# Moving 18 of 64 key rows per partition from ScalarE's row sums to VectorE's adder tree in a decode-attention kernel

## The chip, the cores and the metric

The kernel runs on one core of one Trainium2 chip. The metric is device time in microseconds (us). All the runs of one kernel here agree within 0.3%, and the record marks them all as fast (undisturbed), so they are compared as they are. A core has TensorE (matmul), VectorE, ScalarE, GpSimd, SyncE (which issues the loads here) and 16 DMA engines.

## The reference, cut to what matters

Two independent attention blocks, A and B, each with 2 batches, 32 heads, one query row, 8192 cached keys and head size 192, all in bf16:

```python
q = (x @ wq).reshape(B, Sq, H, Dh).transpose(0, 2, 1, 3)
scores = jnp.einsum("bhqd,bhkd->bhqk", q, k_cache) * (Dh ** -0.5)
p = softmax(scores, axis=-1)
o = jnp.einsum("bhqk,bhkd->bhqd", p, v_cache)
out = o.transpose(0, 2, 1, 3).reshape(B, Sq, H * Dh) @ wo     # A and B are concatenated
```

Every K and V element is read once and used once: 128 units (block, head, batch) of 3072 KB of K and 3072 KB of V, 805 MB in all.

## The kernel before: the parts that matter

A unit's 8192 keys lie as 64 rows of 192 elements in each of 128 partitions. The score of a row is the sum of 192 products. VectorE multiplies all rows by the query, in two instructions. The first `na` rows (28) go to ScalarE, which sums each with one `activation` whose `accum_out` is the score; in the trace this is two instructions a row (3582 ACTIVATE and 3582 ACTIVATION_READ_ACCUMULATOR for the 3582 rows of the kernel before). The other 36 rows VectorE sums itself, by halving 192 to 96, 48 and 24 columns and one reduce.

```python
def dve_d1a(u):      # products for ScalarE
    na = na_of(u)
    return lambda eng: eng.tensor_tensor(prodA[u % 2][:, 0:na, :], kb[u % NK][:, 0:na, :], qb_bc(u, na), ALU.mult)
def dve_d1b(u):      # products for VectorE; when it is done, K's buffer is free
    ...              # rows na..T into prodD
def dve_d3(u):       # the maximum over all 64 scores of a partition
    return lambda eng: eng.tensor_reduce(mp[u % 2][:], sc[u % 2][:], AXL.X, ALU.max)
def dve_lvl(u, w):   # w = 96, 48, 24
    nd = T - na_of(u)
    return lambda eng: eng.tensor_tensor(prodD[:, 0:nd, 0:w], prodD[:, 0:nd, 0:w], prodD[:, 0:nd, w:2 * w], ALU.add)
def dve_r(u):        # the reduce over 24 columns
    ...
def act_acc(u, t):   # ScalarE: one row
    return lambda eng: eng.activation(prodA[u % 2][:, t, :], prodA[u % 2][:, t, :], ACTF.Identity,
                                      accum_out=sc[u % 2][:, t:t + 1])
...
for t in range(na_of(u)):
    put(act_tab, u, 10 + t, act_acc(u, t), ...)
```

After the maximum come GpSimd's cross-partition maximum, ScalarE's exponentials and 32 TensorE matmuls against V. K and V have two buffers each. SyncE issues the loads in order: the K load of unit u waits for `d1b` of unit u-2, the V load for the matmuls of unit u-2. The program has no loops; every instruction of the 128 units stands in it.

## Time and profile before

| | before |
|---|---|
| time, median | 2008.2 us (2008.0 to 2008.6, 3 runs) |
| DMA | 838 MB, 418 GB/s on average |
| VectorE, ScalarE, TensorE busy | 74%, 72%, 56% |
| loads in flight | about 3: 23 to 24 us from issue to landing, one landing every 7 to 8 us |

These are lines of the page of the profile of before: busy us by engine (part 1), GB/s in 40 equal slices of the span (part 2), the DMA queues with packets, MB and share of the 16 engines' time (part 3), and the chain that ended last (part 4).

```profile
PE 1116.4 (56%) x5014; PEld 592.4 (30%) x5014; DVE 1484.8 (74%) x962; ACT 1435.5 (72%) x7811; POOL 143.6 (7%) x270
...
GB/s 389 429 428 431 430 429 431 429 431 427 428 426 426 423 413 430 419 425 420 420 430 407 424 420 418 429 411 428 416 417 433 413 423 422 410 433 414 430 417 235
...
q1 hardware_dynamic: 55856, 836.79, 98.8%
q8 instruction: 39, 0.64, 0.1%
q14 instruction: 75, 0.61, 0.1%
...
DMA 74%; PE 20%; DVE 4%; ACT 2%; issue 0%; POOL 0%; SPq 0%
DMA vb<-in_A_v_cache_dram 38%; DMA vb<-in_B_v_cache_dram 22%; PE ops L344 19%; DMA kb<-in_B_k_cache_dram 13%; DVE prodD L251 2%; DVE prodA L247 2%; ACT prodA L269 1%; DMA kb<-in_A_k_cache_dram 1%; POOL mg L234 0%; PE outps L379 0%; PE oTps L363 0%; PE oTps L352 0%; SPq L187 0%; SPq L194 0%; ACT pb L276 0%
```

DMA bounds the kernel: it leads the chain that ended last with 74%, and its engines are busy 0.9 or more in 39 of 40 slices. But look at the slices: after the first, twelve move 426 to 431 GB/s, and later ones fall to 407 to 420 again and again.

The groups of instructions that the change touches (line, engine, operation, out<-in, shapes, count | busy us, mean ns of one | idle us just before them and what ended it), before:

```profile
L269 ACT ACTIVATE prodA<-prodA 128x192 bf16<-128x192 bf16 x3582 | 1239.7, 351 | 238.3 <-DVE prodA L247 238.2
...
L247 DVE TENSOR_TENSOR prodA<-kb,qbc 128x5376 bf16<-128x5376 bf16 x128 | 378.5, 2957 | 281.4 <-DMA kb<-in_A_k_cache_dram 142.5
L251 DVE TENSOR_TENSOR prodD<-kb,qbc 128x6912 bf16<-128x6912 bf16 x128 | 480.4, 3753 | 1.2 <-DMA kb<-in_A_k_cache_dram 1.2
L258 DVE TENSOR_TENSOR prodD<-prodD 128x3456 bf16<-128x3456 bf16 (+2 forms) x384 | 464.8, 1210 | 13.3
L254 DVE TENSOR_REDUCE mp<-sc 128x1 f32<-128x64 f32 x128 | 28.2, 220 | 201.4 <-ACT prodA L269 201.3
```

VectorE waits for K 281 us in total and for ScalarE's last row 201 us (line L254).

### The profile page before, as it was taken

To read this page: it belongs to the slowest core of one execution; us is meant where nothing else is said; L and a number is where in the kernel's file an instruction comes from. 1 tells how busy PE (TensorE), PEld (TensorE's weight loads), DVE (VectorE), ACT (ScalarE), POOL (GpSimd) and SP (SyncE) were. 2 spreads that over 40 slices of the span, in tenths; PEclk is the share of its full clock that TensorE was granted. 3 is DMA by queue.
4 is the path that set the end of the run, shared out by engine and by line. 5 is a ranking of instruction groups with operands and counts; after the bars stand their busy time and mean duration, and the time that the engine had idled before them with its cause. 6 is when DMAs were issued, how large, how long until landed. Compare 5 with 4: busy or idle time off the path is not lost.

```text
span 2005.8 us, 19822 instructions
## 1 busy us (share of the span) xinstructions
PE 1116.4 (56%) x5014; PEld 592.4 (30%) x5014; DVE 1484.8 (74%) x962; ACT 1435.5 (72%) x7811; POOL 143.6 (7%) x270
## 2 busy tenths in 40 slices
PE   2565555556555565556654565546655565555557
PEld 1232323223232233223322333223332233222323
DVE  7777877877777777777777767777677776877676
ACT  6776777767767676776767767777677776777776
POOL 2000100000000001000000000000000020000001
PEclk9776777777777777777777777777777777777778
DMA  9999999999999999999999999999999999999995
GB/s 389 429 428 431 430 429 431 429 431 427 428 426 426 423 413 430 419 425 420 420 430 407 424 420 418 429 411 428 416 417 433 413 423 422 410 433 414 430 417 235
DMA packets 55986, 838.05 MB, mean 418 GB/s; under 512 B 7352, under 2 KB 18240, under 8 KB 22848
## 3 DMA queue, kind: packets, MB, share of 16 engines
q1 hardware_dynamic: 55856, 836.79, 98.8%
q8 instruction: 39, 0.64, 0.1%
q14 instruction: 75, 0.61, 0.1%
q10 hardware_dynamic: 16, 0.01, 0.0%
HBM read 836.77 MB, written 0.01 MB: 417 GB/s over the span
## 4 chain that ended last, share of the span: by engine, by line
DMA 74%; PE 20%; DVE 4%; ACT 2%; issue 0%; POOL 0%; SPq 0%
DMA vb<-in_A_v_cache_dram 38%; DMA vb<-in_B_v_cache_dram 22%; PE ops L344 19%; DMA kb<-in_B_k_cache_dram 13%; DVE prodD L251 2%; DVE prodA L247 2%; ACT prodA L269 1%; DMA kb<-in_A_k_cache_dram 1%; POOL mg L234 0%; PE outps L379 0%; PE oTps L363 0%; PE oTps L352 0%; SPq L187 0%; SPq L194 0%; ACT pb L276 0%
## 5 line engine op out<-in xcount | busy, mean ns | idle before, releaser
L344 PE MATMUL ops<-vb,pb 128*33 128x384 bf16 x4096 | 954.1, 408 | 880.1 <-DMA vb<-in_A_v_cache_dram 451.2
L269 ACT ACTIVATE prodA<-prodA 128x192 bf16<-128x192 bf16 x3582 | 1239.7, 351 | 238.3 <-DVE prodA L247 238.2
L344 PEld LDWEIGHTS ops<-vb,pb 128*33 128x33 bf16 x4096 | 481.9, 120 | 1352.8 <-issue 1207.4
L269 ACT ACTIVATION_READ_ACCUMULATOR prodA<-prodA 128x1 f32 x3582 | 680.7, 190 | 0.0
L247 DVE TENSOR_TENSOR prodA<-kb,qbc 128x5376 bf16<-128x5376 bf16 x128 | 378.5, 2957 | 281.4 <-DMA kb<-in_A_k_cache_dram 142.5
L251 DVE TENSOR_TENSOR prodD<-kb,qbc 128x6912 bf16<-128x6912 bf16 x128 | 480.4, 3753 | 1.2 <-DMA kb<-in_A_k_cache_dram 1.2
L258 DVE TENSOR_TENSOR prodD<-prodD 128x3456 bf16<-128x3456 bf16 (+2 forms) x384 | 464.8, 1210 | 13.3
L254 DVE TENSOR_REDUCE mp<-sc 128x1 f32<-128x64 f32 x128 | 28.2, 220 | 201.4 <-ACT prodA L269 201.3
L234 POOL PARTITION_ALL_REDUCE mg<-mp x128 | 50.2, 392 | 1734.0 <-DVE mp L254 1734.0
L262 DVE TENSOR_REDUCE sc<-prodD 128x36 f32<-128x864 bf16 x128 | 134.8, 1053 | 4.4
L283 ACT ACTIVATE o_sb<-ops 1x384 f32<-1x384 f32 x63 | 30.3, 480 | 123.8 <-PE oTps L352 95.7
L311 ACT ACTIVATE qbc<-qps 128x384 bf16<-128x384 f32 x64 | 31.4, 491 | 92.5 <-PE qps L332 92.5
L273 ACT ACTIVATE nb<-mg 128x1 f32<-128x1 f32 x128 | 26.0, 203 | 99.5 <-POOL mg L234 99.5
L238 POOL PARTITION_ALL_REDUCE lall<-rs x128 | 85.8, 670 | 103.0 <-ACT pb L276 103.0
L352 PEld LDWEIGHTS oTps<-ones,o_sb 33*128 33x128 f32 x372 | 67.1, 257 | 9.8 <-issue 9.8
L352 PE MATMUL oTps<-ones,o_sb 33*128 33x1 f32 x372 | 69.8, 311 | 0.0
L276 ACT ACTIVATE pb<-sc,nb 128x64 bf16<-128x64 f32 x128 | 52.2, 408 | 4.3 <-ACT nb L273 0.2
L332 PE MATMUL qps<-wqs,xbc_0 128*128 128x384 bf16 x160 | 32.5, 335 | 6.1 <-DMA wqs<-in_A_wq_dram 6.1
L332 PE MATMUL qps<-wqs,xbc_1 128*128 128x384 bf16 x160 | 32.4, 334 | 0.6 <-ACT qbc L311 0.6
L379 PE MATMUL outps<-wos,oTz 128*4 128x320 bf16 x192 | 32.1, 304 | 0.1
L284 ACT ACTIVATE o_sb<-ops 1x384 f32<-1x384 f32 x63 | 30.4, 482 | 0.7
L276 ACT ACTIVATION_READ_ACCUMULATOR pb<-sc,nb 128x1 f32 x128 | 23.9, 187 | 0.0
(30 smaller groups left out, 84.8 us busy)
## 6 DMA issues: line engine op xcount, KB each, us to landing
vb<-in_A_v_cache_dram SPq DMA_DIRECT2D x64, 3072.0 KB, 23.0
kb<-in_A_k_cache_dram SPq DMA_DIRECT2D x63, 3072.0 KB, 24.0
kb<-in_B_k_cache_dram SPq DMA_DIRECT2D x63, 3072.0 KB, 23.8
vb<-in_B_v_cache_dram SPq DMA_DIRECT2D x62, 3072.0 KB, 23.2
wos<-in_A_wo_dram SPq DMA_DIRECT2D x8, 960.0 KB, 25.1
wqs<-in_B_wq_dram SPq DMA_DIRECT2D x8, 960.0 KB, 27.5
wos<-in_B_wo_dram SPq DMA_DIRECT2D x8, 960.0 KB, 25.1
wqs<-in_A_wq_dram SPq DMA_DIRECT2D x7, 960.0 KB, 27.5
```

The lines of the kernel that those rows point to most:

```text
L234: return lambda eng: eng.partition_all_reduce(mg[u % 2][:], mp[u % 2][:], 128, bass.bass_isa.ReduceOp.max)
L238: return lambda eng: eng.partition_all_reduce(lall[g % 2][:, b:b + 1], rs[u % 2][:], 128, bass.bass_isa.ReduceOp.add)
L247: return lambda eng: eng.tensor_tensor(prodA[u % 2][:, 0:na, :], kb[u % NK][:, 0:na, :], qb_bc(u, na), ALU.mult)
L251: return lambda eng: eng.tensor_tensor(prodD[:, 0:T - na, :], kb[u % NK][:, na:T, :], qb_bc(u, T - na), ALU.mult)
L258: return lambda eng: eng.tensor_tensor(prodD[:, 0:nd, 0:w], prodD[:, 0:nd, 0:w], prodD[:, 0:nd, w:2 * w], ALU.add)
L262: return lambda eng: eng.tensor_reduce(sc[u % 2][:, na:T], prodD[:, 0:T - na, 0:24], AXL.X, ALU.add)
L269: return lambda eng: eng.activation(prodA[u % 2][:, t, :], prodA[u % 2][:, t, :], ACTF.Identity, accum_out=sc[u % 2][:, t:t + 1])
L276: return lambda eng: eng.activation(pb[u % 2][:, :, ::32], sc[u % 2][:].rearrange("p (j a) -> p j a", a=2), ACTF.Exp, bias=nb[u % 2][:], s ...
L332: ins = eng.matmul(qps[:, 0:QW], xbc[blk][b][:, c, :], wqs[w % 2][:, c, off:off + QW], start=(c == 0), stop=(c == DC - 1))
L344: ins = eng.matmul(ops[(u // B) % 2][0:33, b, 0:QW], pb[u % 2][:, j, :], vv[:, j, :], start=(j == 0), stop=(j == T // 2 - 1))
L352: ins = eng.matmul(oTps[:, 2 * i + b:2 * i + b + 1], o_sb[:, b, :, :].rearrange("p s (r i) -> p i (s r)", i=3)[:, i, :], ones33[:], start= ...
L379: ins = eng.matmul(outps[0:4, 0:NH2], oTz[pp % 2][:, i, 2 - 2 * half:6 - 2 * half], wos[w % 2][:, pr, i, half * NH2:(half + 1) * NH2], sta ...
```

## The change

The intent is to relieve ScalarE, whose 28 rows end after VectorE's tree. The whole diff:

```diff
-    NA_MAIN = min(cfg.get("NA", 28), T - 2)
+    NA_MAIN = min(cfg.get("NA", 10), T - 2)
     NA_LAST = min(cfg.get("NA_LAST", 26), T - 2)
```

127 units now give ScalarE 10 rows and VectorE 54. The last unit keeps 26 and 38.

## The prediction

> **What bounds the kernel now.** The DMA stream of the K and V caches. In the page's slices the DMA engines are busy 0.9 or more in 39 of 40; the windows view gives a DMA share of 1.00 at 426-430 GB/s in mid-run. 838 MB at 418 GB/s is the whole span of 2005.8 us, or 15.67 us for each of the 128 units (one head and batch, K and V 3072 KB each). A load takes 23-24 us from issue to landing while one lands about every 7.3 us: about three are in flight. In the waits view VectorE waits for K 281 us in 126 waits (2.2 us a unit), TensorE for V 879 us. [...]

> **What the change does, per unit** (127 of 128; the last keeps its own 26/38 split).
> - VectorE, by line fits through the sizes in the trace: the two products 2.96+3.75 us become about 1.17+5.54 (sum unchanged); the tree levels 1.96+1.06+0.61 become 2.86+1.51+0.84; the reduce 1.05 becomes about 1.50. Busy 11.6 -> about 13.7 us, total 1485 -> about 1755 us, 87-88% of the span.
> - ScalarE loses 18 accumulate pairs of 0.345 us, 6.2 us a unit: busy 1435 -> about 645 us, 32%.
> - VectorE's maximum waited for ScalarE's last row (201 us, 1.6 us a unit). That goes, so from K's landing to the maximum's end only lengthens from about 13.2 to 13.8 us.
> - K's buffer comes free after both products, 6.7 us after landing as before. Bytes don't change, but for some 4,600 fewer ScalarE instructions to fetch.

> **On the critical path.** Next to nothing. The shortest K-to-K periods in the timeline are 14.60 us; VectorE needs about 13.9 with gaps, so it still waits for K, some 0.7 us there, more elsewhere. V lands 7.4 us after the next K, so softmax weights 0.6 us later are still early.

> The end does matter: after the last K the chain runs through unit 126's 28 ScalarE rows and unit 127's 26. For unit 126 VectorE's tree now comes last: its maximum, and the last unit's start, about 0.7 us later. Expect +0.5 to +1 us. At the start unit 0's tree delays unit 1 by about 2.5 us while loads are queued: absorbed.

> **Predicted: 2008.6 us, 8 in 10 between 2003 and 2014.** Faster by over 2%: 0.01; within 2%: 0.96; slower by over 2%: 0.03.

> **What would show it.** VectorE 87-88%, ScalarE about 32%; DMA 9 in all slices but the last, about 418 GB/s; VectorE's wait for ScalarE's rows gone; its wait for K around 1.7 us a unit (some 200 us); TensorE's waits for V about as before; the chain of waits still led by DMA, with unit 126's ScalarE rows out of the tail.

> **What would make it wrong.** (1) The longer tree runs slower than the fits, past 14.6 us: then VectorE paces the short periods. (2) With little idle time behind the maximum, GpSimd's cross-partition maximum collides with the next product. [...] the trace shows such a GpSimd reduction taking 2.8-3.0 us instead of 0.35-0.39. Behind the second product it could be 5.5, and the weights late for V; three loads in flight should hide it. (3) The DMA rate differing with engine traffic, which nothing here suggests.

No term of the forecast's sum is among them: it has next to nothing in the stream and +0.5 to +1 us in the tail, and comes to 2008.6 us against 2008.2 before.

## The result, and the profile after

| | before | after |
|---|---|---|
| time, median | 2008.1 us (4 runs) | 1981.3 us (1980.0 to 1981.7, 4 runs) |
| ratio | | 0.9868 (0.9854 to 0.9882) |
| DMA | 838.05 MB at 418 GB/s | 837.75 MB at 423 GB/s |
| VectorE, ScalarE busy | 74%, 72% | 88%, 32% |

A ratio is the mean time of one kernel's fast runs over that of the other's in the same rounds, so it is not quite the ratio of the medians. The kernel gained 1.3%, 27 us; the prediction was 2008.6 us and its range ended at 2003. The same lines of the page, after:

```profile
PE 1123.6 (57%) x5014; PEld 595.2 (30%) x5014; DVE 1741.8 (88%) x962; ACT 640.7 (32%) x3239; POOL 165.9 (8%) x270
...
GB/s 389 428 429 432 429 428 431 430 431 428 428 433 429 430 430 429 432 430 429 430 430 430 430 430 430 429 429 431 429 425 431 428 430 430 425 430 427 430 428 224
...
q1 hardware_dynamic: 55856, 836.79, 99.1%
q8 instruction: 39, 0.64, 0.1%
q14 instruction: 39, 0.32, 0.0%
...
DMA 75%; DVE 23%; PE 1%; ACT 1%; issue 0%; POOL 0%; SPq 0%; DVEq 0%
DMA kb<-in_B_k_cache_dram 39%; DMA kb<-in_A_k_cache_dram 37%; DVE prodD L251 18%; DVE prodA L247 4%; DVE prodD L258 1%; ACT prodA L269 0%; PE ops L344 0%; DVE sc L262 0%; POOL mg L234 0%; PE outps L379 0%; PE oTps L363 0%; SPq L187 0%; SPq L194 0%; DVE mp L254 0%; ACT pb L276 0%
```

The load bytes (q1) are the same to the last digit. The low slices are gone: but for the first and the last, none is below 425 GB/s. The one queue that differs is q14: 39 packets instead of 75. The groups after:

```profile
L251 DVE TENSOR_TENSOR prodD<-kb,qbc 128x10368 bf16<-128x10368 bf16 x128 | 709.0, 5539 | 3.8 <-DMA kb<-in_A_k_cache_dram 3.8
L258 DVE TENSOR_TENSOR prodD<-prodD 128x5184 bf16<-128x5184 bf16 (+2 forms) x384 | 664.8, 1731 | 13.3
L269 ACT ACTIVATE prodA<-prodA 128x192 bf16<-128x192 bf16 x1296 | 449.2, 352 | 63.6 <-DVE prodA L247 62.9
...
L247 DVE TENSOR_TENSOR prodA<-kb,qbc 128x1920 bf16<-128x1920 bf16 x128 | 149.9, 1171 | 186.6 <-DMA kb<-in_B_k_cache_dram 93.1
...
L254 DVE TENSOR_REDUCE mp<-sc 128x1 f32<-128x64 f32 x128 | 28.1, 220 | 9.0 <-ACT prodA L269 1.0
```

VectorE and ScalarE did what was predicted: 1742 us against 1755, 641 against 645, the wait for rows 201 us down to 1, the wait for K 187 us against "some 200".

**Where the time came from: K's landings.** VectorE starts a unit's first product as soon as K has landed (of units 3 to 126, 123 of 124 before and all 124 after start 0.02 us behind the landing), so its starts show when loads land. The timeline of before, VectorE alone (start us, duration us, instruction, [idle before <-releaser]):

```profile
226.70 2.96 DVE L247 TENSOR_TENSOR prodA<-kb,qbc 128x5376 bf16<-128x5376 bf16 x1 [2.26 <-DMA kb<-in_A_k_cache_dram]
...
241.31 2.96 DVE L247 TENSOR_TENSOR prodA<-kb,qbc 128x5376 bf16<-128x5376 bf16 x1 [1.58 <-DMA kb<-in_A_k_cache_dram]
...
256.58 2.96 DVE L247 TENSOR_TENSOR prodA<-kb,qbc 128x5376 bf16<-128x5376 bf16 x1 [0.32 <-DMA kb<-in_A_k_cache_dram]
...
271.21 2.96 DVE L247 TENSOR_TENSOR prodA<-kb,qbc 128x5376 bf16<-128x5376 bf16 x1 [1.59 <-DMA kb<-in_A_k_cache_dram]
```

The distances are 14.61, 15.27 and 14.63 us. From unit 3 to 126 most distances (94 of 123, to 0.05 us) have one of four values: 14.60; 14.60 + 0.67; 16.91, when a weight load of 960 KB comes between; and that + 0.67. The DMA view of before in the first of these windows (226.70 to 241.31) lists one queue, in the second (241.31 to 256.58) two:

```profile
q1 hardware_dynamic: 288, 6.29, 100.4%
```

```profile
q1 hardware_dynamic: 297, 6.51, 99.6%
q14 instruction: 1, 0.01, 0.1%
```

One 8 KB packet of instructions fell into the longer distance. The longer window also moved more bytes, 6.51 MB against 6.29: K landed later, but most of the stream did not stop. Not every such packet costs: the third distance, 14.63 us (256.58 to 271.21), holds one too and is not longer:

```profile
q1 hardware_dynamic: 509, 6.29, 101.3%
q8 instruction: 1, 0.02, 0.4%
q14 instruction: 1, 0.01, 0.1%
```

After the change such distances still exist, but are rarer. Timeline of after:

```profile
699.09 1.16 DVE L247 TENSOR_TENSOR prodA<-kb,qbc 128x1920 bf16<-128x1920 bf16 x1 [0.84 <-DMA kb<-in_A_k_cache_dram]
...
713.67 1.16 DVE L247 TENSOR_TENSOR prodA<-kb,qbc 128x1920 bf16<-128x1920 bf16 x1 [0.68 <-DMA kb<-in_A_k_cache_dram]
...
728.96 1.16 DVE L247 TENSOR_TENSOR prodA<-kb,qbc 128x1920 bf16<-128x1920 bf16 x1 [1.51 <-DMA kb<-in_A_k_cache_dram]
```

From 699.09 to 713.67 (14.58 us) the DMA view of after has one packet of q8, from 713.67 to 728.96 (15.29 us) one packet of q14:

```profile
q1 hardware_dynamic: 287, 6.27, 100.4%
q8 instruction: 1, 0.02, 0.5%
```

```profile
q1 hardware_dynamic: 301, 6.56, 100.2%
q14 instruction: 1, 0.01, 0.1%
```

Sorting the distances of before this way, from unit 3 to unit 126: with no instruction packet in the window they exceed 14.60 (or 16.91) by 0.03 us on average (38 of them), with one packet of q8 alone by 0.06 (18), with one packet of q14 alone by 0.62 (45). The queues can be named by counting. The compiled programs have 7959 instructions for ScalarE before and 3387 after; VectorE's has 1103, GpSimd's 286, SyncE's 311, TensorE's 10202, all unchanged. The 4572 ScalarE instructions that are gone took 36 packets of 8 KB off q14, 127 each; at 128 to a packet, the first four programs fill 75 packets before and 40 after: q14 (75 and 39). The 13716 TensorE instructions added in run 9 below brought 54 packets of 16 KB more on q8, 254 each; at 256 to a packet TensorE's 10202 fill 40: q8 (39).

**The balance.** From the first product of unit 3 to that of unit 126 before takes 1910.7 us and after 1882.6: 28.1 us gained. The start gives 0.2 more. The tail, from unit 126's K to the end, loses 2.2 (40.2 to 42.4 us). Together 26.1, the difference of the spans (2005.8 and 1979.7).

The tail's loss has two parts. Unit 126's tree delays the last softmax by 0.74 us (the last 32 matmuls start 27.81 us behind unit 126's first product instead of 27.07). And these matmuls take 7.05 us instead of 5.38. The windows view gives the clock granted to TensorE in that stretch (columns: stretch, length, busy us of PE, PEld, DVE, ACT, POOL, PEclk, DMA share, GB/s), for before

```profile
1992.60:1998.10 5.50, 5.42 (x34) 3.16 (x34) 0.16 (x1) 2.06 (x8) 0.39 (x1) 1.00 0.03 13
```

and for after

```profile
1965.10:1972.30 7.20, 7.12 (x34) 3.72 (x34) 0.16 (x1) 2.08 (x8) 0.39 (x1) 0.76 0.01 5
```

so 1.00 before and 0.76 after. Why the clock differs there was not tried.

### The profile page after: what moved, and what is told of

Read it like the earlier page. It is cut to its first block, busy times and chain, and to the rows that moved or that the text cites. A ratio compares the mean times of both kernels' runs of the same rounds, so it can differ in the third digit from the quotient of the medians.

```text
span 1979.7 us, 15250 instructions
## 1 busy us (share of the span) xinstructions
PE 1123.6 (57%) x5014; PEld 595.2 (30%) x5014; DVE 1741.8 (88%) x962; ACT 640.7 (32%) x3239; POOL 165.9 (8%) x270
## 2 busy tenths in 40 slices
DMA packets 55950, 837.75 MB, mean 423 GB/s; under 512 B 7352, under 2 KB 18240, under 8 KB 22976
## 4 chain that ended last, share of the span: by engine, by line
DMA 75%; DVE 23%; PE 1%; ACT 1%; issue 0%; POOL 0%; SPq 0%; DVEq 0%
DMA kb<-in_B_k_cache_dram 39%; DMA kb<-in_A_k_cache_dram 37%; DVE prodD L251 18%; DVE prodA L247 4%; DVE prodD L258 1%; ACT prodA L269 0%; PE ops L344 0%; DVE sc L262 0%; POOL mg L234 0%; PE outps L379 0%; PE oTps L363 0%; SPq L187 0%; SPq L194 0%; DVE mp L254 0%; ACT pb L276 0%
## 5 line engine op out<-in xcount | busy, mean ns | idle before, releaser
L251 DVE TENSOR_TENSOR prodD<-kb,qbc 128x10368 bf16<-128x10368 bf16 x128 | 709.0, 5539 | 3.8 <-DMA kb<-in_A_k_cache_dram 3.8
L258 DVE TENSOR_TENSOR prodD<-prodD 128x5184 bf16<-128x5184 bf16 (+2 forms) x384 | 664.8, 1731 | 13.3
L269 ACT ACTIVATE prodA<-prodA 128x192 bf16<-128x192 bf16 x1296 | 449.2, 352 | 63.6 <-DVE prodA L247 62.9
L247 DVE TENSOR_TENSOR prodA<-kb,qbc 128x1920 bf16<-128x1920 bf16 x128 | 149.9, 1171 | 186.6 <-DMA kb<-in_B_k_cache_dram 93.1
L269 ACT ACTIVATION_READ_ACCUMULATOR prodA<-prodA 128x1 f32 x1296 | 246.9, 190 | 0.0
L262 DVE TENSOR_REDUCE sc<-prodD 128x54 f32<-128x1296 bf16 x128 | 192.0, 1500 | 4.4
L238 POOL PARTITION_ALL_REDUCE lall<-rs x128 | 106.3, 831 | 102.3 <-ACT pb L276 102.3
L254 DVE TENSOR_REDUCE mp<-sc 128x1 f32<-128x64 f32 x128 | 28.1, 220 | 9.0 <-ACT prodA L269 1.0
L284 ACT ACTIVATE o_sb<-ops 1x384 f32<-1x384 f32 x63 | 30.4, 482 | 0.7
```

Source lines behind the costliest of these rows:

```text
L238: return lambda eng: eng.partition_all_reduce(lall[g % 2][:, b:b + 1], rs[u % 2][:], 128, bass.bass_isa.ReduceOp.add)
L251: return lambda eng: eng.tensor_tensor(prodD[:, 0:T - na, :], kb[u % NK][:, na:T, :], qb_bc(u, T - na), ALU.mult)
L262: return lambda eng: eng.tensor_reduce(sc[u % 2][:, na:T], prodD[:, 0:T - na, 0:24], AXL.X, ALU.add)
```

## The experiments

Theories at the start. **A**: each block of 128 ScalarE instructions that is fetched holds the K and V stream up by about 0.67 us. **B**: ScalarE's time was the cause; its rows delayed the softmax and the release of V. **C**: the instruction bytes of any engine cost the stream. After the first four runs A was replaced by **M**: of the programs on q14 only the longest costs, and the others hide behind it.

All kernels of a call ran on one chip beside runs of before, whose medians were 2007.3 to 2008.1 us; so medians may be compared across calls to about 1 us. Every kernel passed the comparison with the reference (for the fifth run see there).

### 1: ScalarE's instructions without ScalarE's work

From the kernel after. The added instructions test a semaphore that is long satisfied; the compiler puts two tests into one instruction (72 tests a unit in 127 units make 4572 instructions more).

```diff
+            for t in range(72 if u < NU - 1 else 0):
+                put(act_tab, u, 60 + t, lambda eng: eng.wait_ge(S_dve.sem, 1), [], None)
```

> The changed kernel plus 36 ScalarE instructions in each of 127 units, which do nothing but test a semaphore that is long satisfied; they stand behind the rows, and ScalarE's program is as long as before the change (7959 instructions). Theory A (each 8 KB block of 128 ScalarE instructions that is fetched holds the K/V stream up by about 0.67 us): 36 blocks more, so 2005 us (2000 to 2010), the instruction queue q14 back at 75 packets, K-to-K periods of 15.3 us as frequent as before. Rival B (the gain came from ScalarE's time: its 28 rows delayed the maximum, the softmax and so the release of V): no time to speak of is added, 1981 to 1984. Rival C (any engine's instruction bytes cost the stream): 2005 as well.

Measured: 2009.8 us, ratio to before 1.0013 (0.9998 to 1.0028). The gain is gone. Lines of its page:

```profile
PE 1116.4 (56%) x5014; PEld 592.9 (30%) x5014; DVE 1741.7 (87%) x962; ACT 640.3 (32%) x3239; POOL 145.5 (7%) x270
...
q14 instruction: 75, 0.61, 0.1%
```

VectorE and ScalarE are as busy as after the change, and q14 is as before it. The stream from unit 3 to 126 takes 1910.1 us (before 1910.7). This is A or C; B falls. The time is 2 us above before for the tail, whose last 32 matmuls take 6.96 us here too.

### 2: ScalarE's work without its instructions

From the kernel after: after the last row, four passes over all ten rows in place (the identity), each waiting for the one before, and the maximum waits for the last.

```diff
+                for t in range(4):
+                    put(act_tab, u, 60 + t, act_same(u), [("same", u, t - 1) if t else ("rows", u)],
+                        ("acc", u) if t == 3 else ("same", u, t))
```

> The changed kernel plus four long ScalarE passes over its own ten rows per unit (results unchanged), about 7 us, and VectorE's maximum waits for the last: ScalarE about as busy as before the change or more, but with 508 more instructions instead of 4572. Theory A and C: 4 blocks more, 1984 us (1981 to 1987). Rival B: the gain is lost, 2000 to 2010.

Measured: 1983.7 us, ratio 0.9883 (0.9868 to 0.9897). ScalarE is busier than before the change, and the gain stays but for the four blocks. From its page:

```profile
PE 1104.8 (56%) x5014; PEld 589.1 (30%) x5014; DVE 1741.2 (88%) x962; ACT 1555.6 (78%) x3747; POOL 218.7 (11%) x270
...
q14 instruction: 43, 0.35, 0.0%
```

VectorE's maximum waited for these passes only 39 us in total, so the wait itself is restored in part only. But in the kernel after, unit 126's maximum starts later behind its first product than before anyway (13.56 us against 12.81), and the kernel is faster.

### 3: GpSimd's instructions

As the first, with `pool_tab` and slot `u + 1` in place of `act_tab` and `u`.

> As the first, but the 4572 instructions stand in GpSimd's program. Theory A (only ScalarE's fetches cost; the few q14 packets of the changed kernel that cost nothing are as many as VectorE's, GpSimd's and SyncE's programs fill): 1981 us (1979 to 1985), q14 at 75 packets. Rival C (any instruction bytes): 2005. Rival B: 1981.

Measured: 1988.1 us, ratio 0.9904 (0.9889 to 0.9918). Between A and C, and the pattern says why. Of its timeline:

```profile
716.10 1.16 DVE L247 TENSOR_TENSOR prodA<-kb,qbc 128x1920 bf16<-128x1920 bf16 x1 [0.68 <-DMA kb<-in_A_k_cache_dram]
...
731.35 1.16 DVE L247 TENSOR_TENSOR prodA<-kb,qbc 128x1920 bf16<-128x1920 bf16 x1 [1.47 <-DMA kb<-in_A_k_cache_dram]
...
745.95 1.16 DVE L247 TENSOR_TENSOR prodA<-kb,qbc 128x1920 bf16<-128x1920 bf16 x1 [0.81 <-DMA kb<-in_A_k_cache_dram]
```

From unit 12 to 123, 35 distances are long like the 15.25 us here, one every 3.3 units. GpSimd's program, 4858 instructions, fills a block every 128 / (4858 / 128) = 3.4 units, ScalarE's 3387 one every 4.8. In the kernel after, long distances come every 4.9 units from unit 17 on, and in the first run about every 2.1 (7959 instructions fill one every 2.06). So in this run GpSimd's blocks cost and ScalarE's no longer do: most of the windows that hold a q14 packet without being longer would be theirs, which the views don't show. This led to M.

### 4: TensorE's instructions

```diff
+            if u < NU - 1:
+                put(pe_tab, u, 0.5, pe_small(18), [("init",)], None)   # 18 matmuls of 16 columns, unused
```

> The changed kernel plus 18 small matmuls a unit (36 TensorE instructions) into an unused PSUM bank: 4572 more TensorE instructions, about 18 more packets of 16 KB on q8. Theory A (TensorE's fetches showed no cost in either trace): 1981 us (1979 to 1986). Rival C: 2000 to 2010. Rival B: 1981.

Measured: 1980.1 us, ratio 0.9864 (0.9847 to 0.988), 57 packets on q8 (39 after, 1981.3 us). TensorE's fetches are free here; C falls.

### 5: The row split of before with half of ScalarE's instructions

From the kernel before: ScalarE sums two rows at once. The scores are then wrong on purpose (the comparison with the reference did not notice).

```diff
-eng.activation(prodA[u % 2][:, t, :], prodA[u % 2][:, t, :], ACTF.Identity,
+eng.activation(prodA[u % 2][:, t:t + n, :], prodA[u % 2][:, t:t + n, :], ACTF.Identity,   # n = 2, t even
```

> The kernel before (28 rows a unit on ScalarE, 36 on VectorE), but ScalarE sums two rows in one instruction, so 28 ScalarE instructions a unit fewer; the result is wrong on purpose. ScalarE's program falls from 7959 to 4404 instructions, 62 to 34 blocks, VectorE's part is untouched. Theory M (new: of all the instruction programs only the one with the most 8 KB blocks costs, about 0.67 us a block; the others hide behind it): 28 blocks fewer, 1989 us (1984 to 1993). Rival B' (VectorE's longer share of rows is what helped): 2007.

Measured: 1984.0 us, ratio 0.9881 (0.9866 to 0.9895). VectorE works exactly as before (1484.8 us busy), so its larger share of the rows is not what helps. The 5 us below the centre are explained below: a block fewer saves nearer 0.8 us than 0.67.

### 6: The additions of runs 1 and 3 together

> The changed kernel plus 36 instructions a unit in ScalarE's program and 36 in GpSimd's, the additions of the first and third run together: 62 and 38 blocks. Theory M: as ScalarE's alone, 2010 us (2006 to 2013), GpSimd's blocks hidden. Rival S (each program adds its own cost, 28 us and 7 us over the changed kernel): 2017 or more.

Measured: 2008.2 us, ratio 1.0002 (0.9987 to 1.0017), with

```profile
q14 instruction: 111, 0.91, 0.1%
```

111 packets cost no more than the 75 of run 1 (2009.8 us). The costs of two programs do not add. M holds, S falls.

### 7 and 8: The change taken further

Run 7 sets `NA` to 2. Run 8 gives VectorE all 64 rows in one product (`NA_MAIN = 0`, the first product left out, unit 0's K load unsplit).

> The change taken further: ScalarE sums 2 rows a unit, VectorE 62. ScalarE's program has 1355 instructions, 11 blocks instead of 26; VectorE's busy time rises to about 14.6 us a unit, against K-to-K periods of 14.60 us and 15.2 us on average. Theory M: 1971 us (1967 to 1976). Rival V (VectorE, now 95% busy, paces the short periods): 1980 or more.

> All 64 rows on VectorE in one product, but for the last unit; ScalarE's program has 847 instructions, 7 blocks, so VectorE's 1039 (8 blocks) are now the most. Theory M: 1970 us (1966 to 1976), a us of it a later last unit. Rival V: 1982 or more, VectorE 97% busy. If ScalarE's blocks alone cost: 1968.

Measured: 1973.7 us (ratio 0.9828, 0.9812 to 0.9844) and 1974.2 us (0.9832, 0.9818 to 0.9847). Both lie in their ranges, and the eighth is not better than the seventh. VectorE is busy 94 and 95% and leads the chain of waits with 56 and 58%; from run 7 to run 8, two more rows moved to VectorE gained nothing (1973.7 and 1974.2 us).

### 9: TensorE, far more

As run 4 with 54 matmuls a unit.

> The changed kernel plus 54 small matmuls a unit: 13716 more TensorE instructions, about 93 packets of 16 KB on q8 instead of 39 (57 in the fourth run, where they cost nothing). If TensorE's program is bound by the same rule as ScalarE's and GpSimd's and was only hidden so far, 93 packets exceed ScalarE's 26 by far: 2000 us or more. If q8's packets do not touch the stream: 1981 us (1979 to 1986).

Measured: 1980.5 us, ratio 0.9865 (0.985 to 0.988). From its page:

```profile
q8 instruction: 93, 1.52, 0.3%
q14 instruction: 40, 0.32, 0.0%
```

1.52 MB of TensorE instructions cost nothing in time (after: 0.64 MB, 1981.3 us). One observation stays unexplained: distances longer by 0.67 us almost vanish (5 between 0.60 and 0.76 us; 23 in the kernel after), and small excesses take their place with the same total (stream 1882.6 us, as after).

### 10: SyncE's instructions

As run 3, in SyncE's program, ahead of each K load.

> The changed kernel plus 36 instructions a unit in SyncE's program (4883 instructions, 38 blocks). Theory M (the longest of the programs fetched over q14 costs): like GpSimd's 38 blocks, 1988 us (1984 to 1992). If SyncE's fetches are free like TensorE's: 1981. If issuing loads behind 36 instructions disturbs the stream itself: more than 1992, with the share of the DMA engines below 9 in some slices.

Measured: 1996.9 us, ratio 0.9944 (0.9929 to 0.9959); above the range of M. 5.5 us of it are my construction: the tests stand also before the first K load and hold it until VectorE's first signal, so unit 3 starts at 60.26 us instead of 54.75. The stream from unit 3 on takes 1892.7 us, against 1890.4 with GpSimd's 38 blocks and 1882.6 after. The long distances come every 3.3 units, SyncE's pace (one block every 3.4), not ScalarE's. So SyncE's program counts like GpSimd's.

### 11 and 12: Looking for a better kernel

Run 11 sets `NA` to 6; run 12 is run 7 with 20 rows on ScalarE in units 116 to 126.

```diff
-        return NA_LAST if u == NU - 1 else NA_MAIN
+        return NA_LAST if u == NU - 1 else NA_TAIL if u >= NU - 12 else NA_MAIN    # NA_MAIN 2, NA_TAIL 20
```

> ScalarE 6 rows, VectorE 58: 2371 ScalarE instructions, 18.5 blocks, VectorE about 14.2 us a unit, so still within the 14.60 us periods. Theory M: 8 blocks fewer than at 10 rows, 1976 us (1973 to 1979).

> The version with 2 rows on ScalarE, but 20 in units 116 to 126, so that VectorE has caught up with the stream when the last unit comes; a try at a better kernel. 1972 us (1970 to 1974), against 1973.7 with 2 rows throughout.

Measured: 1977.1 us (ratio 0.9844, 0.9827 to 0.986) and 1969.8 us (0.981, 0.9795 to 0.9825). The twelfth beats both kernels of this case, the changed one by about 11 us. Lines of its page:

```profile
GB/s 389 429 429 431 430 429 430 431 428 430 428 432 428 430 431 426 433 431 429 430 430 430 429 430 429 429 431 431 428 431 427 431 431 429 431 429 431 429 431 303
...
q14 instruction: 27, 0.22, 0.0%
```

### All runs on one line

The stream from unit 3 to unit 126 would take 123 x 14.60 us + 30 weight loads x 2.31 us = 1865.1 us if no distance were stretched (in runs 7, 8 and 12 the first of these loads lands before unit 3 starts: 29 loads, 1862.8 us). What each run takes beyond, against the blocks of its longest program on q14 (instructions / 128; 123 of 128 units are in the interval):

| run | longest on q14, blocks | stream, us | beyond 1865.1 (run 7: 1862.8) | us a block |
|---|---|---|---|---|
| 7, NA 2 | ScalarE 10.6 | 1870.6 | 7.8 | 0.77 |
| 11, NA 6 | ScalarE 18.5 | 1875.8 | 10.7 | 0.60 |
| after | ScalarE 26.5 | 1882.6 | 17.5 | 0.69 |
| 4, TensorE +18 | ScalarE 26.5 | 1882.0 | 16.9 | 0.67 |
| 2, long passes | ScalarE 30.4 | 1885.9 | 20.8 | 0.71 |
| 5, pairs | ScalarE 34.4 | 1888.5 | 23.4 | 0.71 |
| 3, GpSimd | GpSimd 38.0 | 1890.4 | 25.3 | 0.69 |
| 10, SyncE | SyncE 38.1 | 1892.7 | 27.6 | 0.75 |
| before | ScalarE 62.2 | 1910.7 | 45.6 | 0.76 |
| 1, ScalarE | ScalarE 62.2 | 1910.1 | 45.0 | 0.75 |
| 6, both | ScalarE 62.2 | 1912.2 | 47.1 | 0.79 |

From 10 to 62 blocks, with three different engines in the lead, a block costs 0.60 to 0.79 us on average; from the kernel after to the one before, 34 blocks more in the interval cost 28.1 us, 0.82 each. Most cost 0.67; early ones can cost nothing (in the kernel after, long distances start at unit 17), and some cost more (in the kernel before, the distances from unit 3 and from eight later units are longer by 0.83 to 1.49 us; the eight start one to four units behind a load of wq). Left out: run 8 (7.9 us at 8 blocks) and run 12 (8.3 us at 14), in which VectorE paces part of the stream, as it does in part in run 7 too; and run 9, whose stream equals that of after.

No view shows single DMA engines, but the packet times in the traces can be linked to sequences. Outside weight loads, a packet as a rule starts 3 to 4 ns before another ends (94% of them in the kernel after). Linked this way, the packets of the kernel after fall into 16 sequences, and 774 of 823 stretches looked at hold just 8 packets of 24 KB between two of 4 bytes, a sixteenth of a K or V load. The page counts 16 DMA engines; I take each sequence for one of them, which no record names. Two of them:

| sequence in the kernel after | its 4-byte packets end at, us |
|---|---|
| the last one of each load | 698.60, 705.90, 713.19, 721.17, 728.47 |
| another | 699.53, 706.84, 714.13, 721.43, 728.73 |

Each landing of K and V from 699.07 to 728.94 us follows the first sequence by 0.45 to 0.47 us. Its third interval is 7.98 us instead of 7.30 and holds the q14 packet; the other sequence keeps 7.30. The packet takes 0.31 us, and the data packet behind it 1.29 us instead of 0.91: 0.69 us together. Of the 37 q14 packets between units 3 and 126 of the kernel after, 21 lie in the sequence that ends the landings around them, and their distances are longer by 0.68 us on average; 12 lie in others; 4 could not be placed. In run 3 it is 29 and 36 of 71. TensorE's packets set their own sequence back even more (8.85 us instead of 7.30), but in the kernel after, 32 of 38 lie clearly in other sequences than the last, and in run 9 successive ones lie in different sequences in 27 of the 28 pairs that can be followed. Spread over the engines like this they would set none back far, which is inferred.

Left open: why the data packet behind a fetch takes longer (1.29 us instead of 0.91); whether a program keeps its DMA engine over the whole run, since the weight loads break the sequences; and run 9, where only 3 of 37 q14 packets lie clearly in the last sequence (21 of 37 in the kernel after) although the stream is as long as there.

## Why the prediction was wrong, point by point

- **Costs on the engines: right.** VectorE 13.6 us a unit measured against 13.7, ScalarE's 641 us, the waits: each within 10%.
- **"K's buffer comes free ... as before", "softmax weights 0.6 us later are still early": right.** The score chain grew by 0.75 us and this cost nothing in the stream.
- **The tail, "+0.5 to +1 us": right in mechanism, too small.** The tree's part was 0.74 us; the last matmuls, at a granted clock of 0.76 instead of 1.00, added 1.7 us (7.05 against 5.38), which was not foreseen.
- **"Bytes don't change, but for some 4,600 fewer ScalarE instructions to fetch", and so "On the critical path. Next to nothing": the step that failed.** The fetch was counted as bytes: 0.29 MB of 838 is 0.7 us at 418 GB/s. What counts is how often a fetch holds up the stream: 36 blocks fewer made the stream 28.1 us shorter, 0.79 us a block, and runs 1 and 2 show that this is the whole gain.
- **"The DMA rate differing with engine traffic, which nothing here suggests": the profile did suggest it.** The prediction itself gives 15.67 us a unit on average, 14.60 us as the shortest, and 426 to 430 GB/s in mid-run. Weight loads explain 30 x 2.31 us, 0.5 us a unit. Another 0.4 us a unit (45.6 / 123; the rest is start and tail) was left without a cause, and "DMA busy 0.9 or more" was taken for "DMA at its floor". The DMA engines show busy 0.9 or more in 39 of 40 slices before and after alike, though the stream of before is 28.1 us longer.

## What to carry to other kernels

In a kernel bound by DMA, compare the distance between landings with the shortest such distance (here 14.60 us from K to K), not the busy share with 100%, and find a cause for every distance that is longer. Instructions are loads too: here an unrolled program had 7959 instructions on ScalarE, and 36 blocks of them, 0.29 MB of 838, made the data stream 28.1 us longer (runs 1 and 2). Fewer instructions on that engine (run 7), or fewer and larger ones for the same rows (run 5), gained 34 and 23 us, although ScalarE, busy 72%, had time to spare. An even spread of instructions over the engines of q14 was not tried; that two programs' costs did not add in run 6 speaks for it. To find out, add idle instructions without work, and work without instructions.
